# First batch's V turned on TensorE, both layers' weights loaded ahead of the second batch, chunk 0's layers moved forward

## The chip, the core and the metric

The kernel runs on one NeuronCore of a Trainium2 chip. The core has TensorE (PE, matrix multiplies into PSUM; the loading of its stationary operand is listed apart as PEld), VectorE (DVE), ScalarE (ACT), GpSimd (POOL) and SyncE (SP), each with its own instruction stream in program order, and sixteen DMA engines. The metric is device time in microseconds for one execution, and lower is better. Before the change, three executions took 333.70, 334.23 and 335.12 us, a median of 334.23.

## What is computed

Sliding-window causal attention over 8 batches of 8 heads, 576 positions and 64 channels, followed by a two-layer block on 4608 tokens:

```python
scores = scale * np.matmul(q, k.transpose(0, 1, 3, 2))
rel = pos[:, None] - pos[None, :]
scores = np.where((rel >= 0) & (rel < 64), scores, -1e9)
attn = softmax(scores)
x = matmul(attn, v).transpose(0, 2, 1, 3).reshape(B * S, H * D)   # 4608 x 512
h = x @ w_in            # 512 -> 2048
g = h - np.tanh(h)
out = g @ w_out         # 2048 -> 512
```

Inputs and output are float32; the kernel computes in bf16 with float32 sums.

## The kernel before

Attention is done for two heads at a time, a *pair*; `g` counts pairs, g = 4 x batch + pair, from 0 to 31. Queries come in nine blocks of 64. With a window of 64, each block needs the 64 keys of its own block and the 64 before, so 128 keys sit on the partitions for every block.

For one pair the steps are these. `load` brings q or k of the two heads to SBUF (96 partitions, six positions on each; POOL's DMAs cast to bf16 on the way). `cast` reorders it on DVE, ACT or POOL. `tr_heads` (straight from the loaded tile) or `tr_rows` (after a cast) turns it with 12 or 6 TensorE transposes and one eviction from PSUM, so that the channels are on the partitions. `tile_scores` multiplies keys by queries for five and then four blocks, and ACT takes the exponential into `pt`. The mask is either added before, by two identity matmuls with the constant `hide` (how = "hide", or a separate call of `hides` and how = "hidden"), or multiplied in after, by DVE with `mask_sb` (how = "mask"). `tile_pv` multiplies the result by V and normalises it on DVE (a reciprocal and a product) into `xs`. `x_tr` turns `xs` into `xT`, the layers' input.

V must lie with 128 keys on the partitions for each block. Before the change this *window* layout, `vw`, is made by DMAs in every batch: `load_v` brings a pair, `cast_v` copies it on DVE into `vb` with a column of ones beside it, `windows_v` moves the even blocks from `vb` to `vw` by five DMAs a batch, and `odd_windows` copies the odd blocks on DVE from halves of the even ones. `vw` has two buffers for the eight batches.

The layers run over nine chunks of 512 tokens. `h`, c, m: `hp_mm` makes one of 16 slices of the hidden layer with four 512 column matmuls, ACT takes the tanh and DVE (`g_sub`) subtracts it into `gT`. `y`, c, m: `yp_mm` does four of the sixteen matmuls of one of four output slices; after each fourth, `y_out` evicts on ACT and stores through SP. In the text h0 and y0 stand for chunk 0's first and second layer, h1 for chunk 1's first.

Nothing is scheduled by a tool. The first batch's attention is written out in order, before the layers. Then a loop over steps `h` follows a table `OPS`, which says which slice is multiplied at a step, and a table filled by `at(h, ...)`, which says what else is put there. At one step the order is: the layer's matmuls and tanh, the items of `at` in order of their entry, then `g_sub`. Before the change h0 has the even steps 0 to 30, h1 the even steps 32 to 62, y0 the steps 64 to 79; from step 80 chunk 2's first layer alternates with chunk 1's second, and so on to the end.

Because each engine takes its instructions in program order, a copy on DVE that waits for a DMA holds everything later on DVE. POOL's queue takes its DMAs in the order of the calls too: in the code before, V of batch 0 (four), q and k of g1 to g3, four of five window DMAs, the first half of `w_in` (L180), V of batch 1, g4, g5, the second half of `w_in`, g6, g7, then batch 1's windows at step 9; `w_out` (L188) is loaded at step 23.

PSUM has eight banks in one tile `ps`; the numbers handed to the helpers are banks. `warm` issues matmuls whose result nobody reads.

```python
for pr in range(NP):                                   # L467
    load_v(0, pr)
make_ident()
load(1, "k", G)
load(1, "q", G)
```

Of the kernel before, what the change touches and what calls it, by code (L numbers as in the profile page):

```python
# [8 lines left out]
BF16 = mybir.dt.bfloat16  # L9
# [6 lines left out]
def kernel(  # L16
# [9 lines left out]
    nc = tc.nc  # L26
# [50 lines left out]
    xs = [const.tile([128, NJ + 1, NP, D], BF16, name=f"xs{i}") for i in range(2)]  # L77

    stage, rows, whole = {}, {}, {}

    def move(eng, o, i):
        if eng is nc.scalar:
            nc.scalar.activation(o, i, ACT.Copy)  # L83
        else:
            eng.tensor_copy(o, i)  # L85

    def load(g, n, eng):

# [7 lines left out]
        eng.dma_start(out=t, in_=(q if n == "q" else k)[b, pr::NP].rearrange("h (p e) d -> p h (e d)", e=E))  # L96
        stage[g, n] = t
# [41 lines left out]
    def load_v(b, pr):  # L139
        if (b, "v") not in whole:  # L140
            whole[b, "v"] = v_pool.tile([PV, H, EV * D], BF16, tag="v", name="vall")
        t = whole[b, "v"][:, pr::NP]
        nc.gpsimd.dma_start(out=t, in_=v[b, pr::NP].rearrange("h (p e) d -> p h (e d)", e=EV))  # L143
        stage[b, pr, "v"] = t
# [31 lines left out]

    w_out_r = moe_w_out.rearrange("(i p r) d -> i p r d", p=128, r=4)

    def load_w_in(i):
        nc.gpsimd.dma_start(out=w_in_sb[i], in_=w_in_r[:, :, 1024 * i:1024 * i + 1024])  # L180

    def w_in_tile(ki, m):
        i = m // 8
# [33 lines left out]
    nc.vector.memset(vb[:, :, :, D], 1.0)  # L217
    for i in range(NK):
        nc.vector.memset(kT[i][:, 0:64], 0.0)
    nc.vector.memset(vw[0][0:64, 0], 0.0)  # L220

    xT = {}

# [263 lines left out]
    for j, eng in ((8, Y), (0, G), (2, G), (4, G), (6, G)):
        windows_v(0, j, eng)
    load_w_in(0)
    for pr in range(NP):  # L490
        load_v(1, pr)
    for g in 4, 5:
        load(g, "k", G)
        load(g, "q", G)
    load_w_in(1)
    for g in 6, 7:
        load(g, "k", G)
        load(g, "q", G)
# [3 lines left out]
    see()
    copy_mask()
    tr_heads(2, "k", 2, V)
    tile_scores(1, 0, (0, 1), "mask")
    tile_scores(1, 1, (4, 5), "mask")
    tr_heads(2, "q", 3, A)
    tr_heads(3, "k", 2, V)
    tile_scores(2, 0, (0, 1), "mask")
    tile_scores(2, 1, (4, 5), "mask")  # L510
    tr_heads(3, "q", 3, A)
    odd_windows(0, 0)
    odd_windows(0, 1)
# [3 lines left out]
    tile_scores(3, 1, (4, 5), "hidden")
    warm(1)
    tile_pv(0, (6, 7))
    tile_pv(1, (2, 3))  # L520
    tile_pv(2, (0, 1))
    tile_pv(3, (4, 5))
    warm(1)
    x_tr(0, 0, 0, 4, 6, A)
    x_tr(0, 0, 4, 9, 7, A)
    warm(3, 2)
    x_tr(0, 1, 0, 4, 3, V)
    x_tr(0, 1, 4, 9, 6, A)
# [12 lines left out]
    for pr in range(NP):
        at(9, load_v, 2, pr)
    for g in 8, 9, 10, 11:
        at(9, load, g, "k", G)
        at(9, load, g, "q", G)
    at(16, cast_pair, 6, V)
    at(16, cast_pair, 7, V)
    at(18, odd_windows, 1, 0)
    at(18, odd_windows, 1, 1)
    for g, t, ka, qa, a, b, eng in ((4, (10, 11, 13, 14), 6, 7, (4, 5), (6, 7), V),  # L550
                                    (5, (13, 14, 16, 17), 2, 3, (4, 5), (6, 7), V),
                                    (6, (17, 18, 20, 22), 2, 3, (4, 5), (4, 5), A),
                                    (7, (20, 22, 24, 26), 3, 3, (4, 5), (4, 5), A),
                                    (8, (34, 35, 37, 39), 3, 5, (4, 5), (4, 5), A),
                                    (9, (38, 39, 42, 44), 3, 6, (4, 5), (4, 5), A)):
        at(t[0], tr_rows, g, "k", ka, eng)
        at(t[1], tr_rows, g, "q", qa, A)
        at(t[2], tile_scores, g, 0, a, "hide" if g in (4, 6, 7) else "mask")
        at(t[3], tile_scores, g, 1, b, "hide" if g in (4, 6, 7) else "mask")
    for pr in range(NP):  # L560
        at(22 + 2 * pr, tile_pv, 4 + pr, (6, 7))
    at(27, x_tr, 1, 0, 0, 4, 3, A)
    at(28, x_tr, 1, 0, 4, 9, 4, A)
    at(30, x_tr, 1, 1, 0, 4, 7, V)
    at(30, x_tr, 1, 1, 4, 9, 4, A)
    at(21, lambda: [cast_v(2, pr) for pr in range(NP)])
    at(31, cast_pair, 8, V)
    at(23, even_windows, 2, G, G, G, G, G)
    at(36, cast_pair, 9, V)
    at(23, load_w_out, 0)  # L570
    at(23, load_w_out, 1)
    at(23, load_all, 3, "q")
    at(23, load_all, 3, "k")
    at(23, load_v_all, 3)
    at(46, cast_pair, 10, A)
    at(53, cast_pair, 11, V)
    at(39, odd_windows, 2, 0)
    at(39, odd_windows, 2, 1, 1, 2)
    at(40, odd_windows, 2, 1, 5, 2)
    at(45, tile_pv, 8, (6, 7))  # L580
    at(49, tile_pv, 9, (6, 7))
    at(53, x_tr, 2, 0, 0, 4, 6, V)
    at(55, x_tr, 2, 0, 4, 9, 7, A)
    at(76, x_tr, 2, 1, 0, 4, 3, V)
    at(78, x_tr, 2, 1, 4, 9, 3, A)
# [103 lines left out]
```

## Time and profile before

| | us |
|---|---|
| median of three executions | 334.23 |
| the profiled execution | 334.17 |
| its span, first to last instruction | 332.4 |
| first matmul of h0 (L383) | 25.12 |
| first matmul of h1 | 50.69 |
| first matmul of chunk 2's first layer | 89.49 |

The profiled execution took 1.8 us more than its span. Its mean granted TensorE clock is 0.984 of full speed; the lower part lies in the first 18 us. A page or an answer of the trace gives each engine's busy time, groups of instructions by line with the mean of one, what ended the idle time before an instruction (`<-`), and the chain of waits, which is followed back from the last instruction. Matmul times include the pipeline: successive 512 column matmuls of `hp_mm` have a mean of 379 ns each in the groups but start 0.216 us apart, 0.864 for four. So the timeline's starts are used here, not the sums of durations. The rows of the table are starts on that timeline.

### The profile page before, as it was taken

To read this page: it belongs to the slowest core of one execution; us is meant where nothing else is said; L and a number is where in the kernel's file an instruction comes from. 1 tells how busy PE (TensorE), PEld (TensorE's weight loads), DVE (VectorE), ACT (ScalarE), POOL (GpSimd) and SP (SyncE) were. 2 spreads that over 40 slices of the span, in tenths; PEclk is the share of its full clock that TensorE was granted. 3 is DMA by queue.
4 is the path that set the end of the run, shared out by engine and by line. 5 is a ranking of instruction groups with operands and counts; after the bars stand their busy time and mean duration, and the time that the engine had idled before them with its cause. 6 is when DMAs were issued, how large, how long until landed. Compare 5 with 4: busy or idle time off the path is not lost.

```text
span 332.4 us, 6239 instructions
## 1 busy us (share of the span) xinstructions
PE 315.9 (95%) x2435; PEld 175.3 (53%) x2435; DVE 199.5 (60%) x342; ACT 185.1 (56%) x339; POOL 110.5 (33%) x163
## 2 busy tenths in 40 slices
PE   6868999899999999999999999999999999999995
PEld 2544565555555655555555555555554444444444
DVE  4578698983257675767676666766665444334400
ACT  3545878872566666656666666555544344444411
POOL 8827597005920845434624493300000000000000
PEclk9599999999999999999999999999999999999999
DMA  8999998993796299384976968978004001000021
GB/s 159 184 173 191 212 161 120 199 190 101 123 198 125 41 163 236 81 118 116 176 133 113 180 142 140 204 126 205 32 34 104 32 34 63 32 34 32 32 97 64
DMA packets 46766, 40.68 MB, mean 122 GB/s; under 512 B 18416, under 2 KB 40048, under 8 KB 46544
## 3 DMA queue, kind: packets, MB, share of 16 engines
q0 software_dynamic: 21344, 20.06, 40.1%
q1 hardware_dynamic: 25184, 19.92, 23.6%
q8 instruction: 19, 0.31, 0.4%
q10 hardware_dynamic: 208, 0.29, 0.3%
q14 instruction: 11, 0.09, 0.1%
HBM read 36.70 MB, written 10.62 MB: 142 GB/s over the span
## 4 chain that ended last, share of the span: by engine, by line
PE 71%; DMA 9%; POOL 7%; DVE 7%; ACT 3%; issue 2%; POOLq 0%; DVEq 0%; ACTq 0%
PE ps L407 34%; PE ps L383 27%; DMA wi<-in_moe_w_in_dram 4%; PE ps L332 3%; DMA kall<-in_k_dram 3%; PE ps L316 3%; DVE xs L343 2%; PE ps L249 2%; DMA vw<-vb 2%; DVE qt L85 2%; POOL qall L96 1%; DVE gT L395 1%; POOL kall L96 1%; POOL vall L143 1%; POOL vb L85 1%
## 5 line engine op out<-in xcount | busy, mean ns | idle before, releaser
L383 PE MATMUL ps<-xT,wi 128*128 128x512 bf16 x576 | 146.8, 379 | 2.9 <-DVE gT L395 1.2
L407 PE MATMUL ps<-w_out_sb,gT 128*128 128x512 bf16 x560 | 140.8, 379 | 0.3 <-ACT ysb L412 0.3
L395 DVE TENSOR_TENSOR gT<-ps,th 128x512 bf16<-128x512 f32 x144 | 98.5, 689 | 68.6 <-ACT th L388 67.2
L388 ACT ACTIVATE th<-ps 128x512 f32<-128x512 f32 x144 | 86.0, 599 | 80.8 <-PE ps L383 77.0
L383 PEld LDWEIGHTS <-wi 128*128 128x128 bf16 x576 | 60.5, 113 | 48.1 <-issue 3.0
L407 PEld LDWEIGHTS <-gT 128*128 128x128 bf16 x560 | 52.2, 98 | 53.0 <-issue 0.8
L318 ACT ACTIVATE pt<-ps 128x384 bf16<-128x384 f32 x66 | 32.3, 489 | 24.1 <-PE ps L316 24.1
L85 POOL COPY vb<-vall 72x1024 bf16<-72x1024 bf16 x24 | 24.7, 1052 | 32.6 <-DMA vall<-in_v_dram 29.8
L343 DVE TENSOR_TENSOR xs<-ps,rc 64x576 bf16<-64x576 f32 x44 | 33.2, 755 | 1.1
L412 ACT ACTIVATE ysb<-ps 128x512 f32<-128x512 f32 x35 | 21.0, 599 | 18.9 <-PE ps L407 18.8
L85 DVE COPY qt<-ps 64x576 bf16<-64x576 bf16 x18 | 13.7, 760 | 24.1 <-ACT qt L83 24.1
L85 POOL COPY qb<-qall 96x768 bf16<-96x768 bf16 x20 | 16.6, 830 | 24.6 <-DVE pt L322 16.4
L332 PEld LDWEIGHTS <-pt 128*128 128x128 bf16 x198 | 16.5, 98 | 15.3 <-DVE pt L322 0.8
L332 PE MATMUL ps<-vw,pt 128*128 128x130 bf16 x198 | 22.0, 220 | 0.4 <-DVE pt L322 0.4
L316 PE MATMUL ps<-qt,kt 128*128 128x128 bf16 x198 | 21.8, 219 | 0.0
L316 PEld LDWEIGHTS <-kt 128*128 128x128 bf16 x198 | 15.4, 98 | 8.9 <-issue 0.3
L85 POOL COPY kb<-kall 96x768 bf16<-96x768 bf16 x20 | 16.6, 828 | 3.0 <-DMA kall<-in_k_dram 3.0
L322 DVE TENSOR_TENSOR pt<-pt,ps 128x1152 bf16<-128x1152 bf16 x22 | 16.4, 745 | 0.8 <-ACT pt L318 0.8
L83 ACT ACTIVATE kt<-ps 128x576 bf16<-128x576 bf16 x22 | 14.4, 654 | 1.6 <-PE ps L249 1.5
L291 ACT ACTIVATE pt<-ps 128x640 bf16<-128x640 f32 (+1 forms) x20 | 12.5, 648 | 2.9 <-PE ps L288 2.9
L96 POOL DMA_DIRECT2D qall<-in_q_dram x15 | 9.9, 662 | 7.9 <-DMA wi<-in_moe_w_in_dram 7.0
L83 ACT ACTIVATE qt<-ps 64x576 bf16<-64x576 bf16 x18 | 11.5, 638 | 1.0 <-PE ps L249 0.9
(79 smaller groups left out, 205.1 us busy)
## 6 DMA issues: line engine op xcount, KB each, us to landing
out_dram<-ysb SPq DMA_DIRECT2D x35, 256.0 KB
vall<-in_v_dram POOLq DMA_DIRECT2D x5, 576.0 KB, 10.7
qall<-in_q_dram POOLq DMA_DIRECT2D x4, 576.0 KB, 11.6
kall<-in_k_dram POOLq DMA_DIRECT2D x4, 576.0 KB, 11.5
kall<-in_k_dram POOLq DMA_DIRECT2D x15, 144.0 KB, 5.4
qall<-in_q_dram POOLq DMA_DIRECT2D x15, 144.0 KB, 5.2
wi<-in_moe_w_in_dram POOLq DMA_DIRECT2D x2, 1024.0 KB, 11.3
w_out_sb<-in_moe_w_out_dram POOLq DMA_DIRECT2D x2, 1024.0 KB, 14.3
```

Source lines behind the costliest of these rows:

```text
L83: nc.scalar.activation(o, i, ACT.Copy)
L85: eng.tensor_copy(o, i)
L96: eng.dma_start(out=t, in_=(q if n == "q" else k)[b, pr::NP].rearrange("h (p e) d -> p h (e d)", e=E))
L316: nc.tensor.matmul(sp[:, i, :], kT[g % NK][:, 64 * j:64 * j + 128], qT[g % NR][:, :, 64 * j:64 * j + 64], start=True, stop=True)
L318: nc.scalar.activation(PT[g % NPT][:, 3 * grp:3 * grp + 3, :], sp, ACT.Exp, scale=scale)
L332: nc.tensor.matmul(ps[:, 5 + grp, 130 * i:130 * i + 130], PT[g % NPT][:, j, :], vw[b % 2][:, j, 2 * pr:2 * pr + 2, :], start=True, stop=True)
L343: nc.vector.tensor_tensor(xo[r, :, :, pr, :], ov[r, :, :, h, 0:D], rc[r].to_broadcast([64, 3, 3, 64]), ALU.mult)
L383: nc.tensor.matmul(hp, w_in_tile(ki, m), chunk_tile(c)[:, :, ki % 2, 64 * (ki // 2):64 * (ki // 2) + 64], start=(ki == 0), stop=(ki == 3))
L388: nc.scalar.activation(th, hp, ACT.Tanh)
L395: nc.vector.tensor_tensor(gT[c][:, m, :], hp, th, ALU.subtract)
L407: nc.tensor.matmul(yp, gT[c][:, m, s * 128:(s + 1) * 128], w_out_sb[:, m, :], start=(m == 0), stop=(m == M - 1))
L412: nc.scalar.activation(ysb, ps[:, yp_bank(c, s), :], ACT.Copy)
```

## The change

The first batch's V no longer passes through `vb` and the window DMAs. It is loaded like q and k (`load_v0`, into memory that `gT` will use later), turned by `tr_heads` so that channels are on the partitions (`vT`, with 64 zero columns ahead), and turned back in overlapping spans of 128 positions by the new `v_spans`: nine transposes for each pair, three to a PSUM bank beside other data, and three evictions into `vw[0]`. The constant columns and zeros of the buffers are set at the start.

The first batch's pairs are then done one after the other up to their `tile_pv`, where before the four `tile_pv` stood together, and all four pairs use `hide`.

POOL loads, in order: V, k and q of batch 0 mixed, `w_in` in three pieces, both halves of `w_out`, V of batch 1, g4 and g5; then at step 19 batch 1's five windows (all by POOL), g6, g7, V of batch 2, g8 and g9; at step 38 batch 2's windows, g10, g11 and batch 3.

h0 takes steps 0 to 15, twelve of the sixteen y0 groups the even steps 16 to 38, h1 the even steps 40 to 70, and the last four y0 groups steps 57, 65, 71 and 72. The second batch's attention moves from steps 9 to 31 to steps 17 to 39. The steps from 80 on stay, but for a step or so at g11 and g12.

```diff
+    scratch = g_pool.tile([128, M, TOK], BF16, tag="gT", name="scratch").rearrange("p m t -> p (m t)")
+    v0 = scratch[0:P, 0:H * E * D].rearrange("p (h c) -> p h c", h=H)
+    vT = scratch[:, H * E * D:H * E * D + NP * (64 + S)].rearrange("p (i c) -> p i c", i=NP)
+
+    def load_v0(pr):
+        nc.gpsimd.dma_start(out=v0[:, pr::NP], in_=v[0, pr::NP].rearrange("h (p e) d -> p h (e d)", e=E))
+        stage[pr, "v"] = v0[:, pr::NP]
...
-    nc.vector.memset(vw[0][0:64, 0], 0.0)
+    nc.vector.memset(vT[:, :, 0:64], 0.0)
+    nc.vector.memset(vw[0][:, :, :, D:D + 1], 1.0)
+    nc.vector.memset(vw[0][0:64, 0, :, D:D + 1], 0.0)
+    nc.vector.memset(vw[1][0:64, 0], 0.0)
+    nc.vector.memset(qT[1], 0.0)
...
+    def v_spans(pr, places, engs):
+
+        for n, ((bank, c0), eng) in enumerate(zip(places, engs)):
+            tp = ps[:, bank, c0:c0 + 192].bitcast(BF16).rearrange("p (j h d) -> p j h d", j=3, h=2)
+            for i in range(3):
+                c = 64 * (3 * n + i)
+                nc.tensor.transpose(tp[:, i].rearrange("p h d -> p (h d)"), vT[:, pr, c:c + 128], ident)
+            move(eng, vw[0][:, 3 * n:3 * n + 3, 2 * pr:2 * pr + 2, 0:D], tp)
...
-        OPS[2 * m] = "h", 0, m
-        OPS[32 + 2 * m] = "h", 1, m
-        OPS[64 + m] = "y", 0, m
+        OPS[m] = "h", 0, m
+        OPS[40 + 2 * m] = "h", 1, m
+        OPS[16 + 2 * m if m < 12 else (57, 65, 71, 72)[m - 12]] = "y", 0, m
...
+    load_v0(0)
     make_ident()
     load(1, "k", G)
     load(1, "q", G)
     make_hide()
+    load_v0(1)
+    load(2, "k", G)
+    load(2, "q", G)
+    load_v0(2)
+    load_v0(3)
+    load(3, "k", G)
+    load(3, "q", G)
     make_seen()
+    load_w_in(0, 0, 512)
+    load_w_in(0, 512, 1024)
+    load_w_in(1)
+    load_w_out(0)
+    load_w_out(1)
+    for pr in range(NP):
+        load_v(1, pr)
+    for g in 4, 5:
...
+    hides(0, (0, 1))
+    tr_heads(0, "v", 6, V)
+    tile_scores(0, 0, (0, 1), "hidden")
     tile_scores(0, 1, (4, 5))
...
     tr_heads(1, "k", 2, V)
+    v_spans(0, SPANS, (V, V, V))
     tr_heads(1, "q", 3, A)
...
+    tile_pv(0, (6, 7))
+    hides(0, (0, 1))
+    tr_heads(1, "v", 2, A)
...
+    for pr, h in enumerate((17, 17, 18, 18)):
         at(h, cast_v, 1, pr, V)
+    at(19, even_windows, 1, G, G, G, G, G)
+    for g in 6, 7:
+        at(19, load, g, "k", G)
+        at(19, load, g, "q", G)
...
+    at(20, cast_pair, 4, V)
+    at(22, cast_pair, 5, V)
+    at(27, odd_windows, 1, 0)
+    at(27, odd_windows, 1, 1)
+    at(28, cast_pair, 6, V)
+    at(30, cast_pair, 7, V)
+    for g, t, ka, qa in ((4, (21, 22, 24, 25), 2, 3), (5, (25, 26, 27, 28), 2, 3), (6, (29, 30, 31, 32), 2, 3),
+                         (7, (32, 32, 34, 35), 2, 3), (8, (40, 41, 42, 43), 3, 2), (9, (42, 43, 45, 46), 3, 2)):
+        at(t[0], tr_rows, g, "k", ka, A)
         at(t[1], tr_rows, g, "q", qa, A)
+        at(t[2], tile_scores, g, 0, (4, 5), "hide" if g in (7, 9) else "mask")
+        at(t[3], tile_scores, g, 1, (4, 5), "hide" if g in (7, 9) else "mask")
+    for g, h in (4, 29), (5, 31), (6, 35), (7, 37), (8, 49), (9, 51):
+        at(h, tile_pv, g, (6, 7))
+    at(34, x_tr, 1, 0, 0, 4, 1, V)
+    at(36, x_tr, 1, 0, 4, 9, 1, A)
+    at(39, x_tr, 1, 1, 0, 4, 2, V)
+    at(39, x_tr, 1, 1, 4, 9, 3, A)
     for pr in range(NP):
...
+        at(38, cast_v, 2, pr, V)
+    at(38, cast_pair, 8, V)
+    at(38, even_windows, 2, G, G, G, G, G)
+    for g in 10, 11:
+        at(38, load, g, "k", G)
+        at(38, load, g, "q", G)
...
     at(46, cast_pair, 10, A)
+    at(52, cast_pair, 11, V)
+    at(45, odd_windows, 2, 0)
```

More of the change, by code (lines that the diff above doesn't have):

```diff
@@ L177, with load_w_in @@
     w_out_r = moe_w_out.rearrange("(i p r) d -> i p r d", p=128, r=4)
-    def load_w_in(i):
-        nc.gpsimd.dma_start(out=w_in_sb[i], in_=w_in_r[:, :, 1024 * i:1024 * i + 1024])
+    def load_w_in(i, lo=0, hi=1024):
+        nc.gpsimd.dma_start(out=w_in_sb[i][:, :, lo:hi], in_=w_in_r[:, :, 1024 * i + lo:1024 * i + hi])
     def w_in_tile(ki, m):
@@ L241, in tr_heads @@
                 nc.tensor.transpose(tp[64 * h:64 * h + 64, e, :], src[:, h, D * e:D * e + D], ident[:P, :P])
-        o = qs[g % 2] if which == "q" else kT[g % NK][:, 64:]
+        o = qs[g % 2] if which == "q" else kT[g % NK][:, 64:] if which == "k" else vT[:, g, 64:]
         move(eng, o.rearrange("c (p e) -> c p e", e=E), tp.rearrange("c e p -> c p e"))
+    def v_spans(pr, places, engs):
[5 more added lines that the diff above has]
+            move(eng, vw[0][:, 3 * n:3 * n + 3, 2 * pr:2 * pr + 2, 0:D], tp)
     def tr(g, which, bank, *engs):
@@ L371 @@
     HID = {}
-    H0_BANKS = 0, 1, 2, 3, 0, 1, 0, 1, 0, 1, 2, 0, 1, 2, 0, 1
     def hp_bank(c, m):
-        return H0_BANKS[m] if c == 0 else (m + 2) % 3 if c == 1 else m % 2
+        return m % 4 if c == 0 else m % 2
     def hp_mm(c, ms, split):
@@ L398, in yp_bank @@
         if c == 0:
-            return s % 2
+            return (0, 1, 0, 2)[s]
         return (0, 2)[s % 2] if c == NC - 1 else 2
@@ L466 @@
     load(0, "k", A)
-    for pr in range(NP):
-        load_v(0, pr)
+    load_v0(0)
     make_ident()
@@ L472 @@
     make_hide()
-    make_seen()
-    for g in 2, 3:
+    load_v0(1)
[5 more added lines that the diff above has]
+    load(3, "q", G)
+    make_seen()
+    load_w_in(0, 0, 512)
[6 more added lines that the diff above has]
+    for g in 4, 5:
         load(g, "k", G)
         load(g, "q", G)
+    SPANS = (2, 288), (3, 288), (4, 256)
     warm(9)
@@ L482 @@
     tr_heads(0, "q", 3, A)
-    for pr in range(NP):
-        cast_v(0, pr, V)
-    tile_scores(0, 0, (0, 1))
+    hides(0, (0, 1))
+    tr_heads(0, "v", 6, V)
+    tile_scores(0, 0, (0, 1), "hidden")
     tile_scores(0, 1, (4, 5))
[L487 to L498, printed above, removed]
     tr_heads(1, "k", 2, V)
+    v_spans(0, SPANS, (V, V, V))
     tr_heads(1, "q", 3, A)
[L502 to L513, printed above, removed]
-    hides(0, (0, 1))
-    hides(1, (4, 5))
-    tile_scores(3, 0, (0, 1), "hidden")
[L517 to L528, printed above, removed]
+    tile_pv(0, (6, 7))
+    hides(0, (0, 1))
+    tr_heads(1, "v", 2, A)
+    tile_scores(1, 0, (0, 1), "hidden")
+    tile_scores(1, 1, (4, 5))
+    tr_heads(2, "k", 3, V)
+    v_spans(1, SPANS, (V, V, A))
+    tr_heads(2, "q", 2, A)
+    hides(0, (0, 1))
+    tile_pv(1, (6, 7))
+    tr_heads(2, "v", 3, A)
+    tile_scores(2, 0, (0, 1), "hidden")
+    tile_scores(2, 1, (4, 5))
+    v_spans(2, SPANS, (V, V, V))
+    tr_heads(3, "v", 2, V)
+    tr_heads(3, "k", 3, A)
+    hides(0, (0, 1))
+    tile_pv(2, (6, 7))
+    tr_heads(3, "q", 2, A)
+    v_spans(3, SPANS, (V, A, V))
+    tile_scores(3, 0, (0, 1), "hidden")
+    tile_scores(3, 1, (4, 5))
+    x_tr(0, 0, 0, 4, 2, A)
+    x_tr(0, 0, 4, 9, 3, A)
+    tile_pv(3, (0, 1))
+    warm(3, 6)
+    x_tr(0, 1, 0, 4, 6, V)
+    x_tr(0, 1, 4, 9, 7, A)
     def cast_pair(g, eng):
@@ L532, in cast_pair @@
         cast(g, "q", eng)
-    at(0, lambda: nc.vector.memset(vw[1][0:64, 0], 0.0))
-    at(0, lambda: nc.vector.memset(qT[1], 0.0))
-    for pr, h in enumerate((0, 1, 3, 5)):
+    at(1, see)
+    at(1, copy_mask)
+    for pr, h in enumerate((17, 17, 18, 18)):
         at(h, cast_v, 1, pr, V)
-    at(9, even_windows, 1, G, Y, G, Y, G)
-    at(6, cast_pair, 4, V)
-    at(9, cast_pair, 5, V)
+    at(19, even_windows, 1, G, G, G, G, G)
+    for g in 6, 7:
+        at(19, load, g, "k", G)
+        at(19, load, g, "q", G)
@@ L541 @@
     for pr in range(NP):
[L542 to L556, printed above, removed]
-        at(t[1], tr_rows, g, "q", qa, A)
-        at(t[2], tile_scores, g, 0, a, "hide" if g in (4, 6, 7) else "mask")
-        at(t[3], tile_scores, g, 1, b, "hide" if g in (4, 6, 7) else "mask")
@@ L560 @@
-    for pr in range(NP):
[L561 to L574, printed above, removed]
@@ L575 @@
-    at(46, cast_pair, 10, A)
[L576 to L585, printed above, removed]
+        at(19, load_v, 2, pr)
+    for g in 8, 9:
+        at(19, load, g, "k", G)
+        at(19, load, g, "q", G)
+    at(20, cast_pair, 4, V)
@@ new lines @@
+    for g, h in (4, 29), (5, 31), (6, 35), (7, 37), (8, 49), (9, 51):
[4 more added lines that the diff above has]
+    at(39, x_tr, 1, 1, 4, 9, 3, A)
+    for pr in range(NP):
+        at(38, cast_v, 2, pr, V)
[4 more added lines that the diff above has]
+        at(38, load, g, "q", G)
+    at(38, load_all, 3, "q")
@@ L587 @@
+    at(38, load_all, 3, "k")
+    at(38, load_v_all, 3)
+    at(40, cast_pair, 9, V)
+    at(46, cast_pair, 10, A)
+    at(52, cast_pair, 11, V)
+    at(45, odd_windows, 2, 0)
+    at(46, odd_windows, 2, 1, 1, 2)
+    at(47, odd_windows, 2, 1, 5, 2)
+    at(55, x_tr, 2, 0, 0, 4, 6, V)
+    at(57, x_tr, 2, 0, 4, 9, 7, A)
+    at(73, x_tr, 2, 1, 0, 4, 3, V)
+    at(75, x_tr, 2, 1, 4, 9, 3, A)
     LOADS = {4: (75, 77, 79), 5: (106, 109, 102), 6: (140, 144, 126), 7: (0, 0, 158)}
-    STEPS = {2: (0, 0, 49, 57), 3: (72, 79, 86, 93), 4: (100, 107, 114, 121), 5: (128, 135, 142, 149)}
+    STEPS = {2: (0, 0, 48, 55), 3: (73, 79, 86, 93), 4: (100, 107, 114, 121), 5: (128, 135, 142, 149)}
```

## The prediction

> **What bounds the kernel now.** I read the page's shares first, then a table of busy time over four stretches that I cut at the layers' own starts, then the timeline around those starts, then what POOL waited for, and last the DMA packets by window.
>
> ```profile
> PE 315.9 (95%) x2435; PEld 175.3 (53%) x2435; DVE 199.5 (60%) x342; ACT 185.1 (56%) x339; POOL 110.5 (33%) x163
> ...
> DMA  8999998993796299384976968978004001000021
> ```
>
> TensorE is the bound almost throughout, and the DMA engines are full only in the first seventh of the span: that is the part the change rewrites.
>
> ```profile
> 0.00:25.10 25.10, 17.49 (x289) 10.52 (x289) 14.97 (x36) 11.41 (x19) 15.98 (x31) 0.80 1.01 172
> 25.10:50.70 25.60, 23.99 (x295) 14.11 (x296) 21.26 (x43) 18.34 (x33) 19.40 (x28) 1.00 1.13 183
> 50.70:89.50 38.80, 36.95 (x334) 20.99 (x332) 25.93 (x49) 25.53 (x50) 17.24 (x26) 1.00 0.85 149
> 89.50:332.40 242.90, 237.45 (x1526) 129.67 (x1523) 137.30 (x217) 129.86 (x239) 57.84 (x80) 1.00 0.52 107
> ```
>
> Columns: stretch, length, then busy us (instructions) of PE, PEld, DVE, ACT, POOL, the granted clock, the DMA share, GB/s. The cuts are the first matmul of chunk 0's first layer (h0), of h1 and of h2. After 89.5 PE is 98% busy and the code is nearly untouched, so whatever h2's start gains or loses goes to the end. The prediction is therefore a forecast of one moment, h2's start, now 89.49.
>
> ```profile
> 12.16 12.91 DMA wi<-in_moe_w_in_dram
> ...
> 51.68 6.05 DMA vw<-vb
> ```
>
> (Chain of waits.) The first half of w_in lands at 25.07 and releases h0; a set of key windows (vw) lands 6 us after its last issue.
>
> ```profile
> 25.36 0.69 POOL L96 DMA_DIRECT2D qall<-in_q_dram  x1 [7.00 <-DMA wi<-in_moe_w_in_dram]
> ...
> 36.04 0.71 POOL L143 DMA_DIRECT2D vall<-in_v_dram  x1 [3.44 <-DMA wi<-in_moe_w_in_dram]
> ```
>
> POOL's 23rd DMA waited for its 15th, the 32nd for its 24th: eight are out at once, in order. Rates of that one queue, from windows with one kind of load:
>
> ```profile
> DMA packets 872, 0.62 MB, mean 155 GB/s; under 512 B 71, under 2 KB 872, under 8 KB 872
> ...
> DMA packets 1190, 0.88 MB, mean 175 GB/s; under 512 B 89, under 2 KB 1187, under 8 KB 1187
> ```
>
> These are 8 to 12 us and 43 to 48 us, almost only q and k loads: without the small ones 200 and 220 packets of 768 bytes a us, so a 144 KB pair load of 192 packets takes 0.87 to 0.96 us; I use 0.95. By the same view V's 1 KB packets go at 154 a us (40 to 41.8), w_in moved 0.63 MB in 29.5 to 32.5 (5.2 us for 1 MB) but 0.52 MB in 15.5 to 19.5 (slower), w_out 1.37 MB in 58 to 65 (5.2 us for 1 MB).
>
> [...] here the clock is 0.50 from 8 to 18 us while PE was busy 1.2 to 2.0 of every 2 us, mostly transposing[...]
>
> **Part 1: V on TensorE.** Gone: four casts (0.4 us each, DVE), five window DMAs (about 2.5 us of queue) and two odd-window copies (0.86 and 0.70). Added for each pair of heads: 12 transposes (0.28 us from start to start at full clock, 0.74 at half, by the same rows for k), an eviction of 576 columns (0.76 DVE, 0.65 ACT), nine 128x128 transposes (0.5 or 0.96) and three evictions of 384. For these no row exists: [...] the 512 column copy takes 0.42 here, so I take 0.35. Also g1 to g3 get the hide matmuls in place of the mask. Walking PE, ACT and DVE in program order with these durations, half clock to 18.2 us: first pair's k at 6.33, its pv at 11.5, second pair's at 17.5, third's at 21, fourth's at 24.6, last norm done 26.2, last x transposes 26.8. So h0 starts near 26.8, not 25.1. [...] if it stays halved throughout, about 30.6. No load holds this: by the sum below the last q of the batch lands at 15.0. The extra memsets end by 3.6, before the first cast at 5.19.
>
> **Part 2: the loads.** From first packets at 4.0: ten pair loads 9.7 us (to 13.7), w_in's first half in two pieces 7 (20.7; it took 7 to 8 us before, slower than the second), second half 5.2 (25.9), w_out 10.4 (36.3), V of batch 1 (576 packets) 3.8 (40.1), k and q of g4 and g5 3.8 (43.9). A load is seen some 1.3 us after its last packets (before, four V loads and the first k end near 4.0 + 3.8 + 0.95 = 8.7, and PE takes that k at 9.76; I allow a little more). w_in never stops h0: landings 18.5, 22 and 27 against uses at 26.8, 30 and 33.7. w_out lands at 37.6, before y0 needs its second half. But the price is at the end of the queue: batch 1's window DMAs stand behind all of it. POOL can issue them from 42 (cast_v waits for V until 41.3), all five now (two went by SP before), 0.55 us of issue each; eight out means that g5's q, ahead of them, waits only for w_out's 37.6. They move after 43.9 and take 5 to 6 us: landed at 50 to 51.5, taken 51. Before, they were issued at 30.2 to 32.6 and landed by 39.9, where POOL's wait for one ends. Behind them come g6, g7 (+3.9), V of batch 2, g8, g9.
>
> **Part 3: the order of the layers.** The 12 y0 groups moved ahead are 12 x 0.864 = 10.4 us of cover. PE from h0: 16 x 0.864 = 13.8 brings 40.6; seven y0 groups 6.0 and g4's and g5's transposes and scores about 2 bring 49 to 50, with waits for casts of g4 and g5 (landings to 45) inside. Then pv of g4 needs the two odd-window copies. They sit on DVE at step 27, wait for the windows (51) and end at 52.5. Queued behind on DVE: mask of g5, the casts of g6, so g6's transposes, ahead of pv on PE, start near 53.4. That is about 3 us of idle PE. After it: five y0 groups 4.3, the rest of batch 1's attention and x transposes 6.6, and waits of about 2 (q of g6 behind y_out on ACT 1.2; the last x move on DVE behind four cast_v and two casts 1.3, less overlaps). h1 starts near 66.3. Before it started at 50.69 with those 12 groups still to do: comparable 61.1. Loss 5.2. The three y_out of those groups (ACT 0.6 each) and their stores come earlier; SP holds nothing else then. A start of h0 anywhere up to about 30 is absorbed, since the windows come later.
>
> From h1 to h2 before: 38.8 less 10.4 = 28.4, of which some 2 us are waits. The same rows serve after, plus one set of hide matmuls (0.68, g9 where it was masked), less one among g4 to g7 (already left out above). New waits: loads of g10, g11 are now issued at step 38 behind batch 2's windows, so their casts on ACT at step 46 wait for landings near 75 with the tanh rows of h1 behind them; the odd-window copies at step 45 hold DVE and the subtractions of h1. I price the two at 0 to 4, take 2, and take the old 2 us of waits as gone. So h2 moves by 5.2 + 0.7 = 5.9; I take off 0.5 for waits after 89.5 that a later start hides (they sum to 1.3). Span 332.4 + 5.4 = 337.8, and with the 1.8 us around the span (334.17 profiled) 339.5. The median shown is 334.23, so no correction.
>
> **Rivals.** A, the above: 339.5, own range 336.5 to 342.5. For it: the queue is full (1.13 share) in just this stretch, and the added 10.4 us of w_out cannot go elsewhere. Against: h0 loses its interleaving waits (some 3 us of 25.6).
> B, faster: PE stays covered. If the windows are in by about 47 (faster w_out, w_in at 5 us a megabyte from the start), pv of g4 is not held; h1 is then bound by PE and g7's chain, about 60, and the 28.4 after it lose a us or two of waits: h2 at 87, so 331.7. The decider is the window landing against step 29, at 50. For it: DMA is relieved of 2.5 us and 31.8 us of PE work stand between h0 and h1. Against: the byte sum.
> C, late and cold: the clock stays halved, h0 at 30.6[...], so PE reaches step 29 at 54.8 and the excess over 53.4 passes through: 341. [...]
> D, half and half: waits of part 3 mostly overlap, h1 at 63 and h2 at 91: 335.7.
>
> **Numbers.** A 0.53, D 0.14, B 0.20, C 0.13. A change under 0.5% (1.7 us) can't be told from none. Faster by more: most of B, 0.17. Within: the rest of B and part of D, 0.07. Slower: 0.76. The range reaches into B and C: 332.3 to 344; about half of B, a third of C and A's tails are left outside.
>
> **What would show it.** Right: h0's first matmul after 25.5; landings of vw near 51 with DVE's copy of vw waiting for them, a PE hole of 2 to 3 us before the first pv of g4, h1 after 64, ACT's cast of k waiting for kall near 75. Wrong: vw landing before 47, or h2 starting before 89.5. [...]

## The result and the profile after

The changed kernel takes 355.17 us (median of four executions, 349.71 to 358.59) against 333.99 for the kernel before. Two of the four, at 358.15 and 358.59, are over 2% above the fastest and count as slow; the ratio of the other two to the kernel before is 1.0501, 95% interval 1.0425 to 1.0578. The profiled execution took 352.19 us with a span of 350.5, so 18.1 us more span than before's 332.4. The prediction's direction was right and its size was not: it had 5.4 us more span. All sums below are made against that one; e6 below repeats it with an even startup and gives 352.92.

The page of the changed kernel, with the shares, the granted clock and the DMA share in 40 slices of 8.8 us:

```profile
span 350.5 us, 6383 instructions
...
PE 319.9 (91%) x2486; PEld 179.2 (51%) x2521; DVE 201.2 (57%) x350; ACT 189.9 (54%) x345; POOL 106.0 (30%) x158
...
PEclk9999995999998999999999999999999999999999
...
DMA  9999599089349556946597696897501400010012
```

TensorE is busy 4 us longer but stands at 91% instead of 95%. The DMA row has holes in the fifth and the eighth slice that before did not have there, and the clock drops in the seventh slice and again in the thirteenth. The table of stretches (columns as before; the cuts are the start of h0, its end, the start of h1 and of h2):

```profile
0.00:25.50 25.50, 18.70 (x378) 12.26 (x380) 14.08 (x38) 13.29 (x22) 15.73 (x30) 1.00 1.08 190
25.50:39.30 13.80, 13.80 (x68) 7.25 (x66) 9.97 (x16) 9.61 (x17) 1.26 (x2) 1.00 1.12 192
39.30:69.35 30.05, 21.91 (x266) 12.57 (x270) 14.36 (x33) 13.16 (x22) 11.16 (x17) 0.83 0.61 98
69.35:106.65 37.30, 28.00 (x284) 16.71 (x284) 25.58 (x48) 23.81 (x46) 21.42 (x32) 1.00 0.70 114
106.65:350.50 243.85, 237.45 (x1502) 130.45 (x1526) 137.22 (x217) 130.01 (x239) 56.45 (x78) 0.99 0.51 104
```

h0 starts 0.4 us later than before and runs without a gap. The loss is in the next two rows: TensorE is idle 8.1 of 30 us and 9.3 of 37.3; in the two stretches of before that answer to them it was idle 1.6 and 1.9. By moments: h1 starts at 69.35, 8.3 later than the comparable 61.06 of before; from h1 to h2 it is 37.30 against a comparable 28.4, so 8.9 more; after h2 0.95 more. That makes 18.1.

The largest single hole, in the timeline (start, duration, engine, line, tiles; in brackets the idle time before and what ended it):

```profile
40.79 1.42 DVE L93 COPY vb<-vall 72x1024 bf16<-72x1024 bf16 x4
...
42.51 0.90 POOL L173 DMA_DIRECT2D vw<-vb  x1 [6.87 <-DVE kb L93]
...
51.52 0.70 DVE L474 COPY vw<-vw 64x2080 bf16<-64x2080 bf16 x1 [3.97 <-DMA vw<-vb]
...
54.15 0.66 PE L290 MATMUL ps<-ident,kb 96*128 96x96 bf16 x6 [3.95 <-DVE kb L93]
```

The windows land at 51.5 and TensorE stands 3.95 us, both about as predicted. But POOL did not issue them late because of the bytes ahead: the view of the DMA queues counts no packet from 40 to 42. POOL waited 6.87 us for VectorE's casts of V (the view names the cast behind them, `kb`), which sit at steps 17 and 18 behind h0's subtractions. The other waits are small and many (TensorE's, 39 to 107 us; total, times, longest):

```profile
PE ps L290 <- DVE kb L93: 4.4, 2, 3.9
PE ps L309 <- ACT qs L91: 1.9, 3, 0.8
PE ps L270 <- ACT qb L91: 1.9, 1, 1.9
PE ps L325 <- DVE xs L331: 1.5, 1, 1.5
PE ps L353 <- DVE pt L343: 1.3, 1, 1.3
PE ps L309 <- ACT pt L312: 1.2, 2, 0.8
PE ps L403 <- DVE xT L93: 1.1, 1, 1.1
```

In the kernel before, the waits for q, the mask and the normed rows from 25 to 89.5 us were these; all of TensorE's waits sum to 3.8 us there and to 16 here:

```profile
PE ps L304 <- DVE xs L310: 0.9, 1, 0.9
PE ps L288 <- ACT qs L83: 0.4, 1, 0.4
PE ps L332 <- DVE pt L322: 0.4, 1, 0.4
```

They are the links of the attention itself (transposed q, exponentials, normed rows), which before had more groups of layer matmuls beside them: from h1 to h2 the attention has 20 groups beside it (16 of h1, four of y0) where before it had 32. Such matmuls, which TensorE does while the attention waits for its other engines, are called cover below.

### The profile page after: what moved, and what is told of

Same layout as the page of the kernel before. It is cut to its first block, busy times and chain, and to the rows that moved or that the text cites. A ratio compares the mean times of both kernels' runs of the same rounds, so it can differ in the third digit from the quotient of the medians.

```text
span 350.5 us, 6383 instructions
## 1 busy us (share of the span) xinstructions
PE 319.9 (91%) x2486; PEld 179.2 (51%) x2521; DVE 201.2 (57%) x350; ACT 189.9 (54%) x345; POOL 106.0 (30%) x158
## 4 chain that ended last, share of the span: by engine, by line
PE 75%; DVE 9%; ACT 5%; DMA 5%; issue 2%; POOL 2%; POOLq 0%; ACTq 0%; DVEq 0%
PE ps L403 31%; PE ps L427 30%; DMA kall<-in_k_dram 4%; DVE xs L364 3%; PE ps L353 3%; PE ps L337 3%; PE ps L270 2%; DVE gT L415 2%; DVE qt L93 1%; DMA kf<-in_k_dram 1%; PE ps L325 1%; PE ps L253 1%; POOL vw L158 1%; PE ps L442 1%; ACT qt L91 1%
## 5 line engine op out<-in xcount | busy, mean ns | idle before, releaser
L427 PE MATMUL ps<-w_out_sb,gT 128*128 128x512 bf16 x526 | 137.4, 384 | 2.3 <-issue 0.7
L93 POOL COPY vb<-vall 72x1024 bf16<-72x1024 bf16 x20 | 20.6, 1053 | 28.0 <-DMA vall<-in_v_dram 28.0
L93 DVE COPY qt<-ps 64x576 bf16<-64x576 bf16 x18 | 13.7, 760 | 24.2 <-ACT qt L91 24.2
L91 ACT ACTIVATE kt<-ps 128x576 bf16<-128x576 bf16 x25 | 16.3, 652 | 9.8 <-PE ps L290 6.9
L93 POOL COPY kb<-kall 96x768 bf16<-96x768 bf16 x20 | 16.5, 827 | 2.0 <-DMA kall<-in_k_dram 2.0
L467 POOL COPY tick<-gT 1x1 bf16<-1x1 bf16 x14 | 2.5, 179 | 32.5 <-DVE gT L415 27.6
```

What stands on the lines that cost most here:

```text
L427: nc.tensor.matmul(yp, gT[c][:, m, s * 128:(s + 1) * 128], w_out_sb[:, m, :], start=(m == 0), stop=(m == M - 1))
```

## The experiments

Two numbers recur: when h0 starts, and the length from there to the start of h2. In the kernel before they are 25.12 and 64.37 us, in the changed one 25.48 and 81.17. Where two runs differ by under 2 us, the reading is from the trace and not from the medians.

**e1_v_alone** keeps V on TensorE and takes loads and order of layers from before.

```diff
-    load_w_in(0, 0, 512)
-    load_w_in(0, 512, 1024)
-    load_w_in(1)
-    load_w_out(0)
-    load_w_out(1)
+    load_w_in(0)
...
-        OPS[m] = "h", 0, m
+        OPS[2 * m] = "h", 0, m
...
+    at(23, load_w_out, 0)
+    at(23, load_w_out, 1)
```

> V of the first batch on TensorE as in the change, with the order of loads and of the layers from before. Theory 1 (late windows of batch 1 leave TensorE idle and cold): no loss here, 331 to 336 us. Theory 2 (the layers moved forward leave the attention of batches 1 and 2 without matmuls beside it): no loss here either, 331 to 336. Theory 3 (the extra transposes and evictions of V cost the time): most of the 17 us stay, 345 or more.

Measured: 340.64 us median, 334.46 to 342.9, too uneven for a ratio. The fastest execution lies in the range of theories 1 and 2, the other three between them and theory 3. The profiled execution starts h0 at 33.14; after that it is the kernel before, 63.7 us to h2. The start is explained under e5.

**e2_weights_ahead** is e1 with all weights loaded ahead of batch 1's V.

```diff
+    load_w_in(1)
+    load_w_out(0)
+    load_w_out(1)
     for pr in range(NP):
         load_v(1, pr)
```

> As the run with V alone, and all weights loaded ahead of batch 1, with the layers' order from before. If the order of loads is what delays batch 1, VectorE's casts of batch 1's V at steps 0 to 5 wait for it until about 36 us with h0's subtractions behind them: some 8 to 11 us over the run with V alone, 341 to 346. If the loads' order costs nothing, within 2 us of it.

Measured: 343.1 us, ratio 1.0252 (1.0208 to 1.0296); h0 at 30.90, 68.1 to h2. That is in the range of the first case but only 2.5 us over e1, which started late itself; e9 settles it.

**e3_windows_early** is the changed kernel with batch 1's casts of V, windows and the next loads at steps 12 and 13; **e4_windows_loads_early** also loads g10 and g11 there.

```diff
-    for pr, h in enumerate((17, 17, 18, 18)):
+    for pr, h in enumerate((12, 12, 13, 13)):
-    at(19, even_windows, 1, G, G, G, G, G)
+    at(13, even_windows, 1, G, G, G, G, G)
```

> The change, with batch 1's casts of V at steps 12 and 13 in place of 17 and 18, and its windows and the loads behind them at step 13 in place of 19. Theory 1: windows land near 45, the hole of 4 us and the halved clock after it go, 343 us or less. Theory 2: the hole goes but later waits take most of it back, 346 to 351.

> As the run with early windows, and q and k of pairs 10 and 11 loaded at step 13 too, ahead of batch 2's windows. Both theories: ScalarE no longer waits for k of pair 10 (a wait that ended at 79.25 in the change), 2 to 3 us less than the run with early windows; if the time is bound by missing cover, less than 1 us.

Measured: 348.43 us, ratio 1.0418 (1.0354 to 1.0482), and 350.39, ratio 1.0365 (1.0291 to 1.0439): not told apart; e3's lies in the range of theory 2. In e3's trace the windows come 3 us earlier, 1.0 us is left of the 3.95 us hole, the clock stays up until h2 (1.00), and h0 to h2 is 75.51 (e4: 75.52). So the late windows and the half clock behind them are worth 5.7 us, and 11.1 of 16.8 remain without them. In e4's trace h1 to h2 is 36.64 against e3's 38.05; its h0 starts late, at 29.10.

**e5_v_warm** is e1 with 16 matmuls of 512 columns at the start instead of 9; **e11_v_warm12** has 12.

```diff
-    warm(9)
+    warm(16)
```

> V on TensorE alone, as in e1_v_alone, with 16 matmuls of 512 columns ahead of the first transposes instead of 9. Clock theory: e1's 5 to 8 us lie in its startup at half clock; [...] so the first matmul of layer 1 starts at 26.5 to 28.5 (e1: 33.14) and the time is 335 to 338, with runs that lie closer together than e1's 334.5 to 342.9. Rival (the added transposes and evictions themselves cost it): the start stays near 31 to 33 and the time at 339 to 343.

> e5 with 12 matmuls at the start instead of 16: layer 1 starts 0.9 us earlier (26.6) [...], and the time is 333.6 to 334.3, no more than the kernel before. If 12 are too few in some executions, some runs are 3 to 7 us longer, and the median is over 335.

Measured: e5 334.74 us, ratio 1.001 (0.9994 to 1.0027); e11 333.7, ratio 0.9978 (0.9959 to 0.9997). The same transposes in the two traces, e1 first, then e5:

```profile
6.23 0.69 PE L253 MATMUL ps<-ident,kb 96*64 96x96 bf16 x12 [0.61 <-ACT kb L91]
6.72 0.68 PE L253 MATMUL ps<-ident,qb 96*64 96x96 bf16 x12
7.97 0.69 PE L253 MATMUL ps<-ident,scratch 96*64 96x96 bf16 x12
```

```profile
8.11 0.45 PE L253 MATMUL ps<-ident,kb 96*64 96x96 bf16 x12
8.39 0.42 PE L253 MATMUL ps<-ident,qb 96*64 96x96 bf16 x12
9.12 0.45 PE L253 MATMUL ps<-ident,scratch 96*64 96x96 bf16 x12
```

Twelve transposes take 0.69 in e1 and 0.45 in e5, and 0.69 in the kernel before at a granted clock of 0.50 (from 12 to 14 us):

```profile
13.14 0.69 PE L241 MATMUL ps<-ident,qall 96*64 96x96 bf16 x12
```

By this, e1's startup ran at half clock until 30.9 us, although it had begun with 9 long matmuls. V on TensorE costs nothing measurable once the clock is up; e11 starts h0 at 25.65 and has the lowest median of the runs here. Its interval ends just below 1, but 0.2% is under the 0.5% that the prediction took as no change.

**e6_after_warm** is the changed kernel with the same 16 matmuls. **e7_after_fill** adds to e6 36 matmuls whose results are not used, at nine steps between 19 and 79; **e8_before_fill** puts the same 36 into the kernel before, at steps 66 to 78.

```diff
+    def fill(bank, n=4):
+        for i in range(n):
+            nc.tensor.matmul(ps[:, bank, :], ident, w_out_sb[:, i, :], start=True, stop=True)
+    for h, bank in (19, 1), (21, 1), (23, 1), (27, 0), (29, 0), (73, 1), (75, 1), (77, 1), (79, 1):
+        at(h, fill, bank)
```

> The changed kernel with the same 16 matmuls at its start. Clock theory: the start of layer 1 is 26.5 to 28.5 in every execution, the time is 351 to 354 and the runs lie within 3 us of each other (the changed kernel's went from 349.7 to 358.6). If the spread has another source, it stays near 9 us.

> e6 with 36 matmuls of 512 columns put between the steps where the attention of batches 1 and 2 stands alone (7.8 us of TensorE work at full clock, results not used). Cover theory: TensorE is idle or at half clock there while latencies run, so the filler fits in the holes and also holds the clock up: at most +2.5 us against e6, perhaps less than nothing. Rival (these stretches are bound by TensorE's own work): +7 to +8 us.

> The kernel before with the same 36 matmuls in its stretch between the layers of chunk 1 and chunk 2, where TensorE was busy all the time (11.5 of 11.5 us from 78 to 89.5). Cover theory: nothing is there to fill, +6.5 to +8 us. If the filler costs under 3 us here too, filler tells nothing about cover.

Measured: e6 352.92 us (351.58 to 353.85), ratio 1.0559 (1.0518 to 1.0601); e7 352.31, 1.0546 (1.0509 to 1.0583); e8 343.55, 1.0271 (1.0232 to 1.031). With an even startup the changed kernel's spread of 9 us is down to 2.3. In sum the filler costs nothing measurable in the changed kernel and 9.4 us before, more than its own 7.8. The stretch from h0 to h2, one line each (length, then TensorE's busy time and the rest as above): e6, e7, e8.

```profile
27.55:108.81 81.26, 63.96 (x615) 36.79 (x620) 49.66 (x96) 46.76 (x85) 33.70 (x51) 0.94 0.72 117
```

```profile
27.38:108.41 81.03, 68.04 (x651) 38.43 (x655) 49.61 (x96) 47.05 (x85) 35.43 (x54) 1.00 0.76 122
```

```profile
23.70:98.52 74.82, 68.99 (x660) 38.70 (x661) 48.20 (x92) 44.65 (x84) 40.66 (x58) 1.00 0.97 163
```

e7 does 36 matmuls more than e6 in the same time, at full clock throughout. The sum hides two parts. From h0 to h1, where 20 of the 36 stand, e6 and then e7:

```profile
27.55:71.68 44.13, 35.96 (x333) 20.08 (x336) 24.09 (x49) 22.84 (x39) 12.21 (x19) 0.88 0.73 118
```

```profile
27.39:68.98 41.59, 36.90 (x353) 20.35 (x356) 24.02 (x49) 22.70 (x39) 12.15 (x19) 1.00 0.78 127
```

With more to do, TensorE gets through this stretch 2.5 us sooner. It was not the bound there, and the half clock, which does not occur with the filler (mean clock 0.88 in e6, 1.00 in e7), had cost time of its own. The other 16 matmuls (3.5 us) stand in the last 5 us ahead of h2 and make h1 to h2 2.3 us longer (39.43 against 37.13), so that place had room for 1.2 us. In the rest of that stretch no filler was tried; there only its idle time, 9.1 us of 37.1 in e6, speaks. e8's filler stands where TensorE was busy 11.5 of 11.5 us: it shows that this place was bound by TensorE, not all of the kernel before.

**e9_weights_warm** is e2 with 16 matmuls at the start.

> e2 (V on TensorE, all weights ahead of batch 1, the order of layers before) with 16 matmuls at the start instead of 9. If e2's time was e5's plus the late windows plus a startup at half clock: layer 1 starts near 27.5 (e2: 30.90), the stretch from there to chunk 2's layer 1 stays at 68.1, against e5's 63.7, and the time is 338 to 340. If the late windows only hid behind the slow startup, the stretch grows to 70 or more and the time is over 341.

Measured: 343.96 us, ratio 1.026 (1.022 to 1.03): e2's time, although h0 starts 4.6 us earlier, at 26.34. h0 to h2 grew to 74.3. The trace has it on VectorE:

```profile
36.71 0.43 DVE L93 COPY vb<-vall 72x1024 bf16<-72x1024 bf16 x1 [10.03 <-DMA vall<-in_v_dram]
37.05 0.68 DVE L416 TENSOR_TENSOR gT<-ps,th 128x512 bf16<-128x512 f32 x1
```

The cast of V waits 10 us for V behind the weights, and h0's subtractions stand behind the cast; TensorE waits 7.8 us for them. The expectation's second case held: V's landing, not the startup, set e2's time. In the old order of layers, weights ahead of V cost 9 us against e5 by the medians and 10.6 from h0 to h2.

**e10_y0_late** is e3 with 16 matmuls at the start and the second half of y0 moved to where TensorE was thin.

```diff
-        OPS[16 + 2 * m if m < 12 else (57, 65, 71, 72)[m - 12]] = "y", 0, m
+        OPS[16 + 2 * m if m < 8 else (57, 65, 71, 72, 74, 75, 76, 78)[m - 8]] = "y", 0, m
```

> e3 (the changed kernel with early windows; stretch from the first layer 1 to chunk 2's layer 1: 75.5 us) with 16 matmuls at the start, and with the second half of chunk 0's layer 2 moved from steps 32 to 38 and 57 to 72 to steps 57 to 78, so that the thin part ahead of chunk 2 has matmuls beside its attention. Cover theory: the same waits, with the cover moved to where there was none; where it is taken from there was little to spare, so the stretch ends at 72 to 75 and the time at 344 to 347. If the thin part ahead of chunk 2 alone carried the loss (4.25 us long, 2.27 busy, and the half clock after it), the stretch falls to 70 to 71. If cover doesn't count, 75.5 stays.

Measured: 351.05 us, ratio 1.0494 (1.0461 to 1.0526); h0 to h2 79.0.

```profile
27.81:106.84 79.03, 65.42 (x622) 37.75 (x619) 49.15 (x96) 46.66 (x85) 36.69 (x54) 0.91 0.76 123
```

None of the three cases. TensorE's idle time is 13.6 us against e3's 14.9, but it is busy 4.8 us longer: after the groups were taken away from steps 32 to 38, the clock was halved for 10.2 us from 58.6 on and for 3.4 more after 79. In e3, with them, it stayed up until h2. The matmuls between were not spare.

**e12_attention_early** tests a theory that the attention is a chain of fixed length, started late. Beside the lines shown, g6's and g7's loads go between the halves of w_out, and the entries of the later attention move forward with it.

```diff
     load_w_in(1)
+    for pr in range(NP):
+        load_v(1, pr)
+    for g in 4, 5:
+        load(g, "k", G)
+        load(g, "q", G)
     load_w_out(0)
...
-    for g, t, ka, qa in ((4, (21, 22, 24, 25), 2, 3), (5, (25, 26, 27, 28), 2, 3), (6, (29, 30, 31, 32), 2, 3),
+    for g, t, ka, qa in ((4, (11, 12, 13, 14), 6, 7), (5, (14, 15, 16, 17), 6, 7), (6, (20, 21, 22, 24), 2, 3),
```

> The changed kernel's order of layers (h0's sixteen groups in a row, w_out ahead of chunk 1), with 12 matmuls at the start, but with batch 1's V, q and k loaded between w_in and w_out, and its attention begun at step 11, beside h0, instead of step 21. In the runs so far the first transposition of g4 comes 5.4 us after the start of h0 (kernel before, e1, e5, e11) or 16.5 to 17 (the changed kernel, e3, e4), and from it to chunk 2's layer 1 it is 58 to 59.5 us in every run without a hole, whatever layer work lies beside. Chain theory (that time is the attention's own; the loss is the later start): g4 at 35 to 37, chunk 2's layer 1 at 94 to 97, time 339 to 342. Cover theory (h0 in a row takes matmuls from the rest, and the waits come back): from g4 on it grows to 64 or more, chunk 2's layer 1 at 100 or later, time 345 or more.

Measured: 345.34 us, ratio 1.0297 (1.024 to 1.0355); g4 at 37.31, h2 at 101.73, 64.4 us apart, 2.0 of them waits for the windows. All three numbers are those of the cover theory, and the chain theory fell: the equal 58 to 59 us of the other runs are not a length of the attention's own. With h0 in a row, beginning the attention 5 us earlier does not end it earlier.

**e13_w_out_early** loads w_out at step 9 on e11; **e14_h0_row** and **e15_y0_early** then each take a part of the new order on that base (the first and the second edit below; e15 moves y0 forward only to between h1's groups, where the change has most of it ahead of h1); **e16_h0_row_alone** is the first edit on e11 itself.

```diff
-        OPS[2 * m] = "h", 0, m
+        OPS[m] = "h", 0, m
...
-        OPS[64 + m] = "y", 0, m
+        OPS[33 + 2 * m] = "y", 0, m
```

> e11 (V on TensorE, 12 matmuls at the start, everything else as before) with w_out loaded right behind batch 1's windows, at step 9 instead of step 23. It is the base of e14 and e15, which need w_out early. Both theories: nothing waits for the transfers behind it for long, 333.5 to 335. If it pushes batch 2's loads onto the path, 336 or more, and e14 and e15 are read against it.

> e13 with only h0's order changed: its sixteen groups in a row, steps 0 to 15 instead of every other step to 30; the attention of batch 1 keeps its step numbers, so its first transposition has ten groups ahead of it instead of five (4.3 us later). Cover theory (what the attention needs after that is latency, which matmuls taken away don't shorten): +3 to +5 us, h0 to h1 28 to 30 instead of 24.9, and the rest as in e13. Rival (TensorE is the bound, the order of its work is neutral): within 1 us of e13.

> e13 with only y0's order changed: its sixteen groups between those of h1 (steps 33 to 63) instead of after them (steps 64 to 79), where the second half of batch 2's attention and the first of batch 3's then stand alone. Cover theory: +5 to +10 us, and TensorE idle or at half clock in the last 15 us ahead of chunk 2. Rival (order neutral): within 1 us of e13.

> e11 (the loads of before, w_out at step 23) with only h0's sixteen groups in a row. In e14 the same edit on e13 took h0 to h1 from 24.9 to 32.1 us, but e13 had a hole behind it (w_out ahead of batch 2's k and q) that hid most of it. Cover theory: without that hole the 7.2 us stay, h1 to h2 is e11's 38.8, and the time is 339 to 342. Rival (the order is neutral, the 7 us come back later): 333 to 335.

Measured: e13 341.99 us (ratio 1.0243, 1.0191 to 1.0296), e14 343.2 (1.0286, 1.0234 to 1.0338), e15 347.79 (1.0416, 1.037 to 1.046), e16 346.52 (1.0376, 1.0338 to 1.0414). None is clean. e14 is only 1.2 us over e13, near its rival's forecast: h0 to h1 grew by 7.1 us, and h1 to h2 shrank by 6.1, as e13's hole of 4.3 us went. In e13 and e15 batch 2's q and k, which stand behind w_out, come late (in e14, with the same loads, POOL's next load waits 5.9 us for w_out). In e16 TensorE stood 5.1 us behind a VectorE copy of k, and in e13 and e15 it stood 4.3 and 5.7 behind such a copy of q or k too. From e16's timeline:

```profile
44.99 4.26 DVE L93 COPY kb<-kall 96x768 bf16<-96x768 bf16 x1
45.01 4.02 POOL L93 COPY vb<-vall 72x1024 bf16<-72x1024 bf16 x4
...
49.31 0.66 PE L290 MATMUL ps<-ident,kb 96*128 96x96 bf16 x6 [5.10 <-DVE kb L93]
```

A VectorE copy that takes 0.35 us elsewhere takes 4.26 while GpSimd casts batch 2's V for 4.02, and TensorE stands 5.1 us behind it. VectorE's record starts 0.02 us first and ends after all four of GpSimd's copies; what held it, the trace does not name. In before GpSimd casts batch 2's V too (VectorE casts V of the earlier batches only), in 4.03 us from 45.19 on, with no VectorE copy of q or k beside it; VectorE's subtractions and products of that time keep their 0.68 and 0.82. e11 casts it on GpSimd as well, and TensorE waits for no copy of q or k there.

**e17_h0_row_clear** and **e18_y0_early_clear** are e16 and e15 with that cast on VectorE, and in e18 w_out behind g11's loads.

```diff
-    at(21, lambda: [cast_v(2, pr) for pr in range(NP)])
+    at(21, lambda: [cast_v(2, pr, V) for pr in range(NP)])
```

> e16 (h0 in a row on e11) with batch 2's V cast by VectorE instead of GpSimd. In e16 a VectorE copy of 0.35 us ran 4.26 us while GpSimd made its four copies of V (4.02 us), TensorE stood for 5.1 us behind it and then ran at half clock for 16 us. Without that collision the hole is gone: 337 to 341. Cover theory: h0 to h1 is still 28 to 31 us against e11's 24.9 and the time is 336.5 or more. Rival (the order is neutral, e16's loss was the collision alone): 333 to 335.

> e11 with y0's groups between h1's instead of after them, w_out loaded behind batch 2's q and k, and batch 2's V cast by VectorE: e15 without its two holes (3.4 us for a late transfer, 4.4 us for the collision with GpSimd). Cover theory: from h1 to h2 it is 42 us or more against e11's 38.8, idle in the last 15 us, and the time 337 to 342. Rival (order neutral): 333 to 335.

Measured: e17 342.76 us, ratio 1.024 (1.02 to 1.0281); e18 343.74, ratio 1.0279 (1.0238 to 1.032). Both lie 9 to 10 us over e11, more than the cover theory's ranges, and far from neutral. With the cast on VectorE, TensorE waits 1.2 us for the copy of k in e17, and in e18 the copies of q and k take 0.35. From h0 to h2 in e11 and in e17:

```profile
25.65:89.35 63.70, 60.67 (x628) 34.96 (x626) 47.21 (x91) 44.61 (x84) 33.61 (x49) 1.00 0.91 151
```

```profile
26.15:98.30 72.15, 65.48 (x626) 37.99 (x626) 48.52 (x95) 45.22 (x84) 32.34 (x48) 0.91 0.91 151
```

The same loads and nearly the same work, with h0's groups moved together (h0's PSUM banks and the engine of that cast differ too): 8.5 us longer, 4.8 of it TensorE busy for longer (the clock was halved for 13.7 us from 47.8 on) and 3.6 idle. 7.1 of the 8.5 come from h0 to h1, where five groups of h0 now stand ahead of batch 1's attention instead of beside it. No wait in it is over 1.2 us. e18 is 9.2 us longer from h0 to h2; w_out's landing costs 3.4 of that, and all of y0 there uses one PSUM bank, so y0's share alone is not settled. From 90 to 98 us, ahead of h2, TensorE is busy 4.35 of 8:

```profile
PE ps L428 <- DMA w_out_sb<-in_moe_w_out_dram: 3.4, 2, 2.3
```

```profile
90.00:94.00 4.00, 1.83 (x29) 1.00 0.43 79
94.00:98.00 4.00, 2.52 (x25) 0.67 1.04 149
```

## Why the prediction was off

The same stretch in the kernel before, in the changed kernel and in e3, whose clock is up and whose windows are nearly in time (VectorE waits 1.4 us for them):

```profile
25.12:89.49 64.37, 60.92 (x625) 35.09 (x626) 47.18 (x90) 43.86 (x82) 36.63 (x53) 1.00 0.96 162
```

```profile
25.48:106.65 81.17, 63.73 (x614) 36.55 (x619) 49.93 (x96) 46.59 (x85) 33.84 (x51) 0.94 0.74 122
```

```profile
25.70:101.21 75.51, 60.66 (x614) 35.18 (x619) 49.34 (x96) 46.47 (x85) 34.26 (x51) 1.00 0.80 130
```

Before, TensorE was busy 60.92 of 64.37 there. e3 has the same 60.7 us of work and 14.9 of idle time instead of 3.5. Its 11.1 us of loss are all idleness.

- **Part 1, h0 near 26.8:** it came at 25.48, because the clock rose before the transposes: the first twelve took 0.45, at 6.16. The evictions of 384 columns took VectorE 0.35, as assumed. That the clock's moment varies from execution to execution (h0 from 25.5 to 33.1 on the same startup code) was not in the sum.
- **Part 2, windows landed at 50 to 51.5, because of the bytes ahead:** right in time (51.5), wrong in cause, so the time was luck. That the loads arrive in the order of issue, as the sums have it, was the author's assumption; before shows it for one: from 16 to 19.5 us 221 of 222 packets were of 2 KB or more, so w_in moved, and the V loads issued behind it from 12.95 on, in packets of 1 KB, did not. The rates taken were too low: batch 1's V had landed by 38.0, not 41.3, and the queue was empty by 40.4. The place of cast_v on VectorE, behind h0's subtractions, held POOL until 42.5, and the five windows then took 9 us, not 5 to 6.
- **Part 3, a hole of about 3 us, h1 at 66.3:** the hole was 3.95, h1 69.35. From the first transposition after the hole to h1 the text has 12.9 us, and 15.2 were measured, in part at half clock (52.1 to 62.4). "A start of h0 anywhere up to about 30 is absorbed" is wrong: the windows and the attention, which begins 16.5 to 17 us after h0, move with it. In e6 h0 starts 2.1 us later than in the changed kernel, the windows are taken 2.3 later and h2 starts 2.2 later.
- **h1 to h2, the step that failed:** "The same rows serve after, plus one set of hide matmuls". It took y0's 10.4 us out of a stretch of 38.8 and kept the waits at 2, which with the hide matmuls asks for TensorE to be busy some 27 of 29.1 us. It measured 37.3, with 28.0 busy: the work was right within 1 us, and the idle time was 9.3 us instead of 2. e3, e4 and e6 repeat it (38.05, 36.64 and 37.13). y0 had not only been work in that stretch: with it went the layer matmuls that stood beside the attention's waits. Work that is taken out of a stretch shortens it only as long as TensorE is the bound. e8 shows that it was so before where y0 stood. Here the traces show it no longer is. No run moved y0 alone to where the change has it, so that y0's going is the cause is argued from the waits and not shown singly. For h0 it is shown: e17, which pulls it together on the old base, is 9 us slower than e11.
- **Waits "0 to 4, take 2":** ACT's cast of k waited for kall until 79.25 (75 predicted), and TensorE 1.88 us behind it. e4, which loads it earlier, has 1.4 us less from h1 to h2. Right in kind and size, and not where the loss was.
- **The rivals:** C, late and cold, had h0 at 30.6, and it came at 25.48; the clock was halved later, for 10.2 us after the hole and for 3.4 at h2, and TensorE's busy time grew by 2.8. B, faster, did not occur: with h0 taken out ahead, the attention's own waits ended last. Nor did D (h1 at 63, h2 at 91). Most of A's signs came, h0 at 25.48 falling just short, but none of them concerned how busy TensorE stays from h1 to h2. A's last sum, 337.8 and 1.8, should read 339.6.

So the 16.8 us from h0 to h2 are: 5.7 for windows that come late and what follows them (e3), and 11.1 of idle time under the new order, put down to lost cover. The exact share of h0's and of y0's new places in the 11.1 stays open: singly, on the old base, moving them cost 8.5 and up to 9.2. Untested is what the attention's other PSUM banks and the other pairs chosen for the mask add; TensorE's waits for exponentials (`ACT pt`), where a shared bank would show, sum to 1.7 us in e3 and 0.4 in e17. That the whole change gains nothing to pay for it is shown by e5 and e11: V on TensorE with the old loads and order, after 16 or 12 matmuls, is within 0.3% of the kernel before.

## What to carry to other kernels

Before subtracting moved work from a stretch, compare what is left with the latencies that it covered: a stretch that is 95% busy (here 36.95 of 38.80 us) may be only just so, with two limits at the same length. Filler that computes nothing is a cheap probe: put it in, and see stretch by stretch whether the time moves, since a gain in one can hide a loss in the next (2.5 us and 2.3 in e7). And when loads are reordered, look at what waits in order behind the instruction that takes the delayed data, on its engine: e9's V, 10 us late at its cast, held back h0's subtractions, not only the attention.

## What the hardware showed that I had not expected

- **The clock of the same startup varies from execution to execution.** By the lengths and starts of its matmuls, TensorE behind the same 9 matmuls was at full clock from 4.3 (the changed kernel), 6.4 at the latest (e3), 16.7 (e4), 24.0 (e2) and 30.9 us (e1) on, with h0 at 25.48, 25.70, 29.10, 30.90 and 33.14. With three more matmuls of 512 columns none of e11's 14 executions came late (333.19 to 335.31); with seven more, one of e5's 20 took 339.98, for a reason that no trace shows. Once full, the clock stayed full through the same transposes: in e5 twelve of them take 0.45 at 8.11 and 0.42 at 21.69.
- **The granted clock can read as full where TensorE is slow.** It reads 1.00 in e1 from 4 to 33.1 us; only the transposes' durations (0.69 against 0.45) tell otherwise.
- **One VectorE copy lasted as long as four GpSimd copies.** In e16 a copy of 0.35 us took 4.26 beside GpSimd's four copies of 4.02, with VectorE's record starting first.
